# Packed queries in another engine order: when weight columns are copied, which accumulators are emptied first, and what lies between two spreads

## The chip, the cores and the metric

The kernel runs on one core of a Trainium2 chip. The metric is device time in microseconds (us), as the median of several executions; lower is better. The engines that matter are TensorE (PE in the profile, its weight loads PEld), ScalarE (ACT), VectorE (DVE), GpSimd (POOL) and SyncE (SP), which issues the DMAs. Each engine works off its own instructions in order.

## The reference

Four layers in a row, all in bf16 with 32-bit sums: linear attention (A), MLP (B), A, B, with the same weights for both A and both B. S = 2048 tokens, D = 576, F = 4608, 32 heads of 18 columns.

```python
phi = lambda t: jnp.where(t > 0, t + 1, jnp.exp(t)) + 1e-6
def A(y):                       # y: layernorm of x
    q, k, v = heads(y @ wqkv)   # 32 heads of 18
    pq, pk = phi(q), phi(k)
    kv = einsum("bhsd,bhse->bhde", pk, v)
    z = einsum("bhsd->bhd", pk)
    den = einsum("bhqd,bhd->bhq", pq, z)[..., None] + 1e-6
    return (einsum("bhqd,bhde->bhqe", pq, kv) / den) @ wo
def B(y):                       # y: layernorm of x
    return gelu(y @ w1 + b1) @ w2 + b2
x = x + A(ln(x)); x = x + B(ln(x)); x = x + A(ln(x)); x = x + B(ln(x))
```

## The kernel before, in words

**Order.** The order of TensorE's instructions is the order in which the program writes them (`pe(...)` chains each to the last). On the other engines a scheduler places the instructions, but manual dependencies (`tc.add_manual_dep(later, earlier, NOSYNC, ...)`, which order two instructions of one engine without a semaphore) and lists of names (`in_order`) fix it around the places at issue. All DMA loads of the beginning are chained on SP's queue. PSUM is cut into four single banks that go round as a ring (`ps_h`, tag "h") and two pairs of banks (`accA`, `accB`) for long sums. A ring tile waits until the last reader of the tile four places earlier is done.

**The attention layer.** It is linear attention without the usual products of values: instead of v it uses x^T phi(k). For each of 16 tiles of 128 tokens the keys are made in two halves of 288 columns (`k_half`, L731), phi is applied by ScalarE and VectorE, and `rows_by_keys` (L773) adds x^T times phi(k) for the first half of the keys into four 128-row blocks (k = 0 to 3, in `accA` and `accB`) and a block of the remaining 64 rows plus a row of sums (k = 4, the "tail", in a ring bank). Between them the queries are made: `q_proj(g, c)` for groups g = 0 to 3 of 128 columns (7 heads of 18 and two more columns) and blocks c of 512 tokens (L699), and for the group 4 of the 64 columns that are left, two blocks packed in one bank (L704).

**Packed queries.** Group 4 has 72 columns. Eight of them fill up the two free columns of each full group, so that a full group has 128: POOL copies them within the weight tile `wqkv_sb` (L240, two copies, called from `load_wq` at the beginning). In layer 0 the layernorm of a tile goes over VectorE's statistics, a power on POOL (`ln_rstd`, L477), two more steps on POOL, and then five transposes on TensorE (L549) with a copy on ScalarE; tiles from `XB` on are transposed by a DMA instead.

**After the last tile** come `last_rows_by_keys` (the tail block and the sums of the second half of the keys), `z_groups`/`z_tail`/`z_products` (the denominators' vectors), and the sums for the second half of the keys (`sums(n)`: n token tiles of `rows_by_keys`, four matmuls of 288 columns each), which are spread as filling between these steps: `den_stage` (L906: denominators of two blocks of 512 tokens), `quad_stage` and `scale_stage` (1/denominator for group 4), `quarter_stage(c)` (L949: 1/denominators of block c spread over the features by 16 small matmuls into all four ring banks, which ScalarE copies, L953, into the single buffer `turned`), `quarter_scale` (L959: VectorE multiplies the queries by it), `kv_groups` (L825: the weights of the values times the emptied sums `k2`, L758 and L756 being the copies that empty them), and `kv_wo_half(g, half)` (L854: kv times the output weights, one ring bank each; for group 4 copied out at L857 to L859, and eight rows of it sent to the other groups by four DMAs). Then `wo_products` (L1092) forms the output of the layer and `residual` (L675) adds x.

**The MLP layer** (L1207, L1271) follows with its own layernorms; `lnp.feed(..., hold=...)` says at which step of the attention layer's end a tile's layernorm may start.

Of the kernel before, what the change touches and what calls it, by code (L numbers as in the profile page):

```python
# [15 lines left out]
P = 128  # L16
NT = S // P
KD = 5
# [22 lines left out]
def build(tc, A_x, A_wqkv, A_wo, B_w1, B_b1, B_w2, B_b2, out, dbg=None, n_layers=4):  # L41
    nc = tc.nc
    dbg = dbg or {}
    with ExitStack() as ctx:
# [116 lines left out]
        XB = 7  # L161
# [68 lines left out]
        def load_wq():  # L230
# [7 lines left out]
            chained(nc.sync.dma_start(out=wqkv_sb[0:64, 4, GF4 * P:QW], in_=A_wqkv[4 * P:D, 0:GO[0]]))  # L238
            for n, ks in ((P, slice(0, 4)), (64, slice(4, 5))):
                nc.gpsimd.tensor_copy(  # L240
                    out=wqkv_sb[0:n, ks, 0:GF4 * P].rearrange("p k (g c) -> p k g c", g=GF4)[:, :, :, 126:P],
                    in_=wqkv_sb[0:n, ks, QW - 2 * GF4:QW].rearrange("p k (g c) -> p k g c", g=GF4))

# [140 lines left out]
        class LNPipe:  # L384
# [11 lines left out]
            def tick(self, transposes=1):  # L396
                land()
                for it in list(self.items):
# [69 lines left out]
                    elif st == 1:  # L468
# [8 lines left out]
                        nc.gpsimd.tensor_tensor(out=rstd[:], in0=it["u"][:], in1=neg_half[:], op=ALU.pow)  # L477
# [207 lines left out]
        def layer_A(li, next_kind, pre_a1=None):  # L685
# [65 lines left out]
            def plus_eps(engine, out, in_, eps):  # L751

                if li > 0:
                    (engine.copy if engine is nc.scalar else engine.tensor_copy)(out=out, in_=in_)
                elif engine is nc.scalar:
                    engine.activation(out=out, in_=in_, func=ACT.Identity, bias=eps)  # L756
                else:
                    engine.tensor_scalar(out=out, in0=in_, scalar1=eps, scalar2=None, op0=ALU.add)  # L758

            def rows_by_keys(t, half, chunks=(4, 0, 1, 2, 3), done=True):  # L760
# [14 lines left out]
                if summed and t == NT - 1:  # L775
# [4 lines left out]
                    for rows_, col in ((slice(0, 64), 4), (slice(64, 65), 5)):  # L780
                        nc.vector.tensor_scalar(out=key_eps[rows_, col:col + 1], in0=self_k["tail"][rows_, HALF:HALF + 1],
                                                scalar1=1e-6, scalar2=None, op0=ALU.mult)
                if 4 in chunks and t == NT - 1:
# [13 lines left out]
                if t < NT - 1:  # L797
                    return
                for i, engine in enumerate((nc.scalar, nc.vector)):
                    for j in range(2):  # L800
                        plus_eps(engine, k2[2 * i + j][:, cols], self_k["acc"][i][:, j, 0:HALF],
                                 key_eps[:, 2 * i + j:2 * i + j + 1])
# [15 lines left out]
            def kv_groups(groups):  # L818
# [3 lines left out]
                for g in groups:  # L822
                    cols = slice(GO[g], GO[g] + GR[g])
                    for k in range(KD):
                        pe(nc.tensor.matmul(ps[0:GR[g], start_of[g]:start_of[g] + GR[g]],  # L825
                                            lhsT=wqkv_sb[:, k, VO + GO[g]:VO + GO[g] + GR[g]],
                                            rhs=k2[k][:, cols], start=(g == groups[0] and k == 0), stop=(k == KD - 1),
# [23 lines left out]
            def kv_wo_half(g, half, by_dve=None):  # L851
# [4 lines left out]
                if g == GF4:  # L856
                    nc.vector.tensor_copy(out=kvwo["rest"][64:72, cols], in_=wp[64:72, 0:HALF])  # L857
                    nc.scalar.copy(out=kvwo[GF4][0:64, cols], in_=wp[0:64, 0:HALF])
# [523 lines left out]
```

## Time and profile before

| | |
|---|---|
| three runs | 760.76, 761.78, 762.96 us; median 761.78 |
| the profiled execution | 760.52 us; its span, first to last instruction, 758.8 us |
| granted TensorE clock | 1.000 over the span |
| busy | PE 745.7 us (98%), ACT 316.0 (42%), DVE 260.8 (34%), POOL 116.0 (15%) |
| attention layer 0, with the start | 0 to 102.18 us, PE busy 94.44 |
| MLP layer 1 | 102.18 to 384.01 us, PE busy 281.83 of 281.83 |
| attention layer 2 | 384.01 to 474.05 us, PE busy 87.64 of 90.04 |
| MLP layer 3 | 474.05 to 758.8 us, PE busy 281.83 of 284.75 |

How to read the rows. A row of the stretch table begins with the stretch in us, then its length, and the busy time with the count of instructions for PE, PEld, DVE, ACT and POOL; then the granted clock, the busy share of the DMA engines and GB/s. A row of the timeline begins with the start and the duration of a group of alike instructions, then engine, line, operation, output<-inputs, shapes and count; in brackets stands the idle time of that engine just before, and what ended it. In the chain, SPq, DVEq and so on are an engine's own queue. A row of the DMA list has destination<-source, the queue, the count and the size of one.

### The profile page before, as it was taken

The numbers are of one execution on the slowest core, as the hardware profiler recorded it, in microseconds if no ns is written. First come the engines' busy times: TensorE is split into PE (matmuls) and PEld (weight loads), VectorE is DVE, ScalarE is ACT, GpSimd is POOL, SyncE is SP. The second block draws the span as 40 slices with busy tenths as digits, with TensorE's granted clock in tenths as the row PEclk, the third lists the DMA queues.
The fourth block names the chain that finished last, engine by engine and source line by source line (L and its number), as shares of the span: only waits on it lengthen the run. The fifth ranks groups of instructions, "written<-read, shape, count | busy, mean of one in ns | idle before, by whom it ended". The sixth has DMA issues, their size and how long they took to land.

```text
span 758.8 us, 15697 instructions
## 1 busy us (share of the span) xinstructions
PE 745.7 (98%) x6531; PEld 474.7 (63%) x6531; DVE 260.8 (34%) x649; ACT 316.0 (42%) x706; POOL 116.0 (15%) x227
## 2 busy tenths in 40 slices
PE   8998999999999999999999999999999999999998
PEld 4665754774477457646776667457646754674476
DVE  6756844136023503401457577600230132000000
ACT  4666646205600650263057666660164036205600
POOL 4830402002000301300100004300020021001000
PEclk9999999999999999999999999999999999999999
DMA  8796694226302711320404137430240033011000
GB/s 224 188 250 138 201 320 143 67 63 188 84 35 83 181 51 48 107 67 21 137 24 118 42 112 273 171 83 16 79 111 20 16 125 83 9 32 56 2 9 24
DMA packets 89218, 75.89 MB, mean 100 GB/s; under 512 B 45674, under 2 KB 73786, under 8 KB 89146
## 3 DMA queue, kind: packets, MB, share of 16 engines
q1 hardware_dynamic: 89146, 74.88, 34.4%
q8 instruction: 51, 0.84, 0.5%
q14 instruction: 21, 0.17, 0.1%
HBM read 48.10 MB, written 24.77 MB: 96 GB/s over the span
## 4 chain that ended last, share of the span: by engine, by line
PE 91%; DVE 3%; ACT 2%; issue 1%; SPq 1%; POOL 1%; DMA 0%; DVEq 0%; POOLq 0%; ACTq 0%
PE m_ps L1271 36%; PE h_ps L1207 21%; PE hp_ps L1207 16%; PE wo_ps L1092 4%; PE k_ps L731 4%; PE q_ps L699 3%; PE k_ps L773 3%; ACT turned L953 1%; PE m_half L1271 1%; DVE pq L959 1%; PE q_ps L704 1%; PE k_tail L773 0%; PE rden_ps L949 0%; DMA wqkv_sb<-in_A_wqkv_dram 0%; SPq L234 0%
## 5 line engine op out<-in xcount | busy, mean ns | idle before, releaser
L1271 PE MATMUL m_ps<-w_sb,hT 128*128 128x288 bf16 x2232 | 274.8, 286 | 0.0
L1271 PEld LDWEIGHTS <-hT 128*128 128x128 bf16 x2304 | 224.3, 98 | 60.4 <-issue 3.4
L1207 PEld LDWEIGHTS <-w_sb 64*128 64x128 bf16 x2304 | 124.5, 94 | 136.4 <-issue 1.9
L1207 PE MATMUL hp_ps<-yT,w_sb 64*128 64x512 bf16 x1152 | 178.0, 376 | 0.0
L1207 PE MATMUL h_ps<-yT,w_sb 64*128 64x512 bf16 x1152 | 147.9, 376 | 0.0
L1212 ACT COPY relay_sb<-relay_sb 128x1 f32<-128x1 f32 x144 | 28.5, 198 | 261.3 <-PE h_ps L1207 218.7
L1203 ACT ACTIVATE hT<-h_ps,b1T 128x512 bf16<-128x512 f32 x144 | 91.1, 684 | 44.2 <-PE h_ps L1207 44.2
L477 POOL TENSOR_TENSOR ln_rstd<-ln_u,neg_half 128x1 f32<-128x1 f32 x62 | 34.8, 562 | 413.1 <-DVE ln_u L459 215.1
L1203 ACT ACTIVATE hT<-hp_ps,b1T 128x512 bf16<-128x512 f32 x144 | 91.2, 693 | 0.0
L675 DVE TENSOR_TENSOR xbf<-m_ps,xo 128x576 bf16<-128x576 f32 x15 | 11.4, 758 | 212.7 <-PE m_ps L1271 212.7
L675 DVE TENSOR_TENSOR xo<-m_ps,xo 128x576 f32<-128x576 f32 x16 | 12.1, 758 | 168.4 <-PE m_ps L1271 168.4
L658 POOL TENSOR_TENSOR xo<-xo,b_bc 128x576 f32<-128x576 f32 x32 | 40.9, 1282 | 105.8 <-DMA xo<-x_d 64.5
L1207 PE MATMUL h_ps<-yT,w_tail 64*128 64x512 bf16 x144 | 54.1, 376 | 0.0
L1207 PE MATMUL hp_ps<-yT,w_tail 64*128 64x512 bf16 x144 | 54.1, 376 | 0.0
L731 PE MATMUL k_ps<-wqkv_sb,yT 128*128 128x288 bf16 x320 | 44.5, 286 | 1.6 <-DMA yT<-x 1.2
L1092 PE MATMUL wo_ps<-kvwo,pq 128*128 128x288 bf16 x320 | 42.3, 286 | 0.0
L699 PE MATMUL q_ps<-yT,wqkv_sb 128*128 128x512 bf16 x160 | 39.6, 379 | 0.2
L731 PEld LDWEIGHTS <-yT 128*128 128x128 bf16 x320 | 30.9, 98 | 12.4 <-DMA yT<-x 1.5
L1207 PEld LDWEIGHTS <-w_tail 64*128 64x128 bf16 x288 | 27.1, 94 | 17.1
L1092 PEld LDWEIGHTS <-pq 128*128 128x128 bf16 x320 | 30.6, 98 | 8.4 <-issue 0.2
L621 ACT ACTIVATE phi_e<-q_ps 128x512 bf16<-128x512 f32 (+1 forms) x38 | 21.6, 574 | 24.2 <-PE q_ps L699 21.8
L340 DVE STREAM_TRANSPOSE turned<-y_ring 128x576 bf16<-128x576 bf16 x40 | 30.3, 766 | 0.4
(162 smaller groups left out, 541.7 us busy)
## 6 DMA issues: line engine op xcount, KB each, us to landing
xo<-x_d SPq DMA_DIRECT2D x48, 288.0 KB
x_d<-xo SPq DMA_DIRECT2D x32, 288.0 KB
xl<-x_d SPq DMA_DIRECT2D x24, 288.0 KB
y_d<-turned SPq DMA_DIRECT2D x40, 144.0 KB
w_sb<-in_B_w_dram SPq DMA_DIRECT2D x6, 864.0 KB
yT<-y_d SPq DMA_DIRECT2D x10, 512.0 KB
w_sb<-in_B_w_dram SPq DMA_DIRECT2D x9, 512.0 KB
x_d<-xn SPq DMA_DIRECT2D x16, 288.0 KB
```

The costliest lines, as they stand in the source:

```text
L340: turn = nc.vector.transpose(out=turned[:, :, j, :], in_=y[:, 0:D])
L477: nc.gpsimd.tensor_tensor(out=rstd[:], in0=it["u"][:], in1=neg_half[:], op=ALU.pow)
L658: nc.gpsimd.tensor_tensor(out=xo[:], in0=xo[:], in1=b2_bc[:], op=ALU.add)
L675: total = nc.vector.tensor_tensor(out=xn[:, cols].rearrange("p (h n) -> p h n", h=2), in0=halves, in1=xo[:, cols].rearrange("p (h n) -> p ...
L699: pe(nc.tensor.matmul(qp[:], lhsT=wqkv_sb[:, k, g * P:(g + 1) * P], rhs=yT[:, k, c * CA:(c + 1) * CA], start=(k == 0), stop=(k == KD - 1)))
L731: pe(nc.tensor.matmul(kp[:, 0:HALF], lhsT=yT[:, k, t * P:(t + 1) * P], rhs=wqkv_sb[:, k, KO + half * HALF: KO + (half + 1) * HALF], start= ...
L773: pe(nc.tensor.matmul(dst, lhsT=lhsT, rhs=pk, start=(t == 0), stop=(t == NT - 1)))
L1092: pe(nc.tensor.matmul(wp[:, half, 0:HALF], lhsT=features, rhs=kvwo[slot][:, half * HALF:(half + 1) * HALF], start=(g == WO_ORDER[0]), stop ...
L1203: act_last["gelu"] = nc.scalar.activation(out=to, in_=ps, func=ACT.Gelu_apprx_tanh, bias=b1T[:, f:f + 1], scale=1.0).ins.name
L1207: mm = pe(nc.tensor.matmul(dst[n], lhsT=wt, rhs=mv, start=(seen[n] == 0), stop=(seen[n] == 8)))
L1212: relay = nc.scalar.copy(out=relay_sb[:, 1:2], in_=relay_sb[:, 0:1])
L1271: pe(nc.tensor.matmul(acc[half][:, 0:cols.stop - cols.start], lhsT=hT[f][:, j * P:(j + 1) * P], rhs=w2_sb[:, f, cols], start=(f == 0), sto ...
```

## The change

- **Weight columns.** The two copies of L240 are taken out of `load_wq` into a function `fill_groups`, which is called later, after `load_wqkv(2)` (the loads of the values' weights) and after the keys of tile 2. Manual dependencies put them behind the last power on POOL and one behind the other, the power of tile 4 behind them, and each power of a layer-0 tile behind POOL's last normalization.
- **XB** goes from 7 to 8: tile 7 is transposed on TensorE.
- **Long accumulators first.** In `rows_by_keys` of the last tile the copies that empty `accA` and `accB` are written ahead of those of the tail, and ScalarE's copies are held in this order.
- **kv by key blocks.** `kv_groups` loops over the key blocks (0, 1, 4, 2, 3) outside and over the groups inside.
- **Denominators.** `den_stage` runs its two blocks inside the loop over the groups.
- **Last group.** `kv_wo_half(4, ...)` copies its 72 rows once, by VectorE, into `rest`, and after the second half POOL copies 64 rows from there to each of the two tiles of group 4. The second spread, `quarter_stage(1)`, stands ahead of `kv_wo_half(4, 0)` instead of behind `kv_wo_half(4, 1)`, and `sums` are dealt out otherwise. `last_rows_by_keys` stands ahead of `z_groups(0, 1)` and `z_tail`.
- **hold** of token tile 2 in the attention layer 2 is 8 instead of 6.

```diff
@@ -158,7 +158,7 @@
         y_ring = [const.tile([P, DPAD], BF16, name=f"y_ring{i}") for i in range(NY)]
         key_eps = const.tile([P, 8], F32, name="key_eps")
         AHEAD = 4
-        XB = 7
+        XB = 8
         BY_ACT = (10, 13)
         turned = const.tile([P, D // 32, TPC, 32], BF16, name="turned")
         x_d = dpool.tile([NT, P, D], F32, name="x_d")
@@ -236,10 +236,14 @@
             chained(nc.sync.dma_start(out=wqkv_sb[:, 0:4, GF4 * P:QW],
                                       in_=A_wqkv[0:4 * P, 0:GO[0]].rearrange("(k p) n -> p k n", p=P)))
             chained(nc.sync.dma_start(out=wqkv_sb[0:64, 4, GF4 * P:QW], in_=A_wqkv[4 * P:D, 0:GO[0]]))
+
+        def fill_groups():
             for n, ks in ((P, slice(0, 4)), (64, slice(4, 5))):
-                nc.gpsimd.tensor_copy(
+                filled = nc.gpsimd.tensor_copy(
                     out=wqkv_sb[0:n, ks, 0:GF4 * P].rearrange("p k (g c) -> p k g c", g=GF4)[:, :, :, 126:P],
                     in_=wqkv_sb[0:n, ks, QW - 2 * GF4:QW].rearrange("p k (g c) -> p k g c", g=GF4))
+                tc.add_manual_dep(filled.ins, first_ones["fill"].ins.name if "fill" in first_ones else pool_last["pow"], NOSYNC, reason="tiles go on first")
+                first_ones["fill"] = filled
 
         nc.scalar.preload_act_table_set("natural_log_exp_and_others")
         load_x0(0)
@@ -474,7 +478,12 @@
                             named(f"re{it['t']}", nc.scalar.activation(out=rstd[:], in_=rstd[:], func=ACT.Exp, scale=-0.5))
                             it["stage"] = 2
                             continue
-                        nc.gpsimd.tensor_tensor(out=rstd[:], in0=it["u"][:], in1=neg_half[:], op=ALU.pow)
+                        power = nc.gpsimd.tensor_tensor(out=rstd[:], in0=it["u"][:], in1=neg_half[:], op=ALU.pow)
+                        pool_last["pow"] = power.ins.name
+                        if it["kind"] == "A" and it["norm"] == "pool" and pool_last["norm"] is not None:
+                            tc.add_manual_dep(power.ins, pool_last["norm"], NOSYNC, reason="tiles one by one")
+                        if it["t"] == 4 and "fill" in first_ones:
+                            tc.add_manual_dep(power.ins, first_ones.pop("fill").ins.name, NOSYNC, reason="queries' weights first")
                     elif st == 2 and it["norm"] != "dve":
                         nmr = work.tile([P, 1], F32, name="ln_nmr", bufs=4)
                         nc.gpsimd.tensor_scalar(out=nmr[:], in0=it["mv"][:, 0:1], scalar1=1.0 if it["stats"] == "act" else -1.0,
@@ -751,11 +760,15 @@
             def plus_eps(engine, out, in_, eps):
 
                 if li > 0:
-                    (engine.copy if engine is nc.scalar else engine.tensor_copy)(out=out, in_=in_)
+                    step = (engine.copy if engine is nc.scalar else engine.tensor_copy)(out=out, in_=in_)
                 elif engine is nc.scalar:
-                    engine.activation(out=out, in_=in_, func=ACT.Identity, bias=eps)
+                    step = engine.activation(out=out, in_=in_, func=ACT.Identity, bias=eps)
                 else:
-                    engine.tensor_scalar(out=out, in0=in_, scalar1=eps, scalar2=None, op0=ALU.add)
+                    step = engine.tensor_scalar(out=out, in0=in_, scalar1=eps, scalar2=None, op0=ALU.add)
+                if engine is nc.scalar:
+                    if act_last.get("k2") is not None:
+                        tc.add_manual_dep(step.ins, act_last["k2"], NOSYNC, reason="banks of the sums first")
+                    act_last["k2"] = step.ins.name
 
             def rows_by_keys(t, half, chunks=(4, 0, 1, 2, 3), done=True):
 
@@ -780,6 +793,11 @@
                     for rows_, col in ((slice(0, 64), 4), (slice(64, 65), 5)):
                         nc.vector.tensor_scalar(out=key_eps[rows_, col:col + 1], in0=self_k["tail"][rows_, HALF:HALF + 1],
                                                 scalar1=1e-6, scalar2=None, op0=ALU.mult)
+                if done and t == NT - 1:
+                    for i, engine in enumerate((nc.scalar, nc.vector)):
+                        for j in range(2):
+                            plus_eps(engine, k2[2 * i + j][:, cols], self_k["acc"][i][:, j, 0:HALF],
+                                     key_eps[:, 2 * i + j:2 * i + j + 1])
                 if 4 in chunks and t == NT - 1:
                     nc.gpsimd.memset(zk[:, cols], 0.0)
                     plus_eps(nc.scalar, k2[4][0:64, cols], self_k["tail"][0:64, 0:HALF], key_eps[0:64, 4:5])
@@ -794,12 +812,6 @@
                     del row_of[t]
                     if li == 0 and t == NT - 1:
                         x0_tiles.clear()
-                if t < NT - 1:
-                    return
-                for i, engine in enumerate((nc.scalar, nc.vector)):
-                    for j in range(2):
-                        plus_eps(engine, k2[2 * i + j][:, cols], self_k["acc"][i][:, j, 0:HALF],
-                                 key_eps[:, 2 * i + j:2 * i + j + 1])
 
             def last_rows_by_keys():
 
@@ -819,12 +831,12 @@
 
                 ps = ps_h.tile([P, 512], F32, name="kv_ps", tag="h")
                 start_of = {g: 126 * i for i, g in enumerate(groups)}
-                for g in groups:
-                    cols = slice(GO[g], GO[g] + GR[g])
-                    for k in range(KD):
+                for k in (0, 1, 4, 2, 3):
+                    for g in groups:
+                        cols = slice(GO[g], GO[g] + GR[g])
                         pe(nc.tensor.matmul(ps[0:GR[g], start_of[g]:start_of[g] + GR[g]],
                                             lhsT=wqkv_sb[:, k, VO + GO[g]:VO + GO[g] + GR[g]],
-                                            rhs=k2[k][:, cols], start=(g == groups[0] and k == 0), stop=(k == KD - 1),
+                                            rhs=k2[k][:, cols], start=(g == groups[0] and k == 0), stop=(k == 3),
                                             skip_group_check=True))
                 full = [g for g in groups if g < GF4]
                 n = len(full)
@@ -854,10 +866,10 @@
                 pe(nc.tensor.matmul(wp[0:GR[g], 0:HALF], lhsT=kvT[0:GR[g], g, 0:GR[g]],
                                     rhs=wo_sb[0:GR[g], g, cols], start=True, stop=True))
                 if g == GF4:
-                    nc.vector.tensor_copy(out=kvwo["rest"][64:72, cols], in_=wp[64:72, 0:HALF])
-                    nc.scalar.copy(out=kvwo[GF4][0:64, cols], in_=wp[0:64, 0:HALF])
-                    nc.vector.tensor_copy(out=kvwo[GF4 + 1][64:P, cols], in_=wp[0:64, 0:HALF])
+                    nc.vector.tensor_copy(out=kvwo["rest"][0:72, cols], in_=wp[0:72, 0:HALF])
                     if half:
+                        for hi in range(2):
+                            nc.gpsimd.tensor_copy(out=kvwo[GF4 + hi][64 * hi:64 * (hi + 1), :], in_=kvwo["rest"][0:64, :])
                         for i in range(GF4):
                             nc.sync.dma_start(out=kvwo[i][126:P, :], in_=kvwo["rest"][64 + 2 * i:66 + 2 * i, :])
                     return
@@ -899,12 +911,13 @@
             def den_stage(c):
 
                 dp = ps_h.tile([P, 512], F32, name="den_ps", tag="h")
-                for i in range(2):
-                    for g in range(G):
+                for g in range(G):
+                    for i in range(2):
                         for j in range(TPC):
                             features, slot = tile_of(g, c + i, j)
                             pe(nc.tensor.matmul(dp[32 * j:32 * (j + 1), i * P:(i + 1) * P], lhsT=zsel[:, slot, :],
-                                                rhs=features, start=(g == 0), stop=(g == G - 1)))
+                                                rhs=features, start=(g == 0 and i == 0), stop=(g == G - 1),
+                                                skip_group_check=True))
                 rden = work.tile([P, 2, P], BF16, name="rden", bufs=1)
                 nc.scalar.activation(out=dp[:, 2 * P:4 * P], in_=dp[:, 0:2 * P], func=ACT.Ln, bias=key_eps[:, 7:8])
                 act_last["rden"] = nc.scalar.activation(out=rden[:].rearrange("p i n -> p (i n)"), in_=dp[:, 2 * P:4 * P],
@@ -981,6 +994,7 @@
                 phi()
                 rows_by_keys(0, 0, (0, 1, 2, 3), done=False)
                 keys(2)
+                fill_groups()
                 feed_and_tick(4, 2)
                 rows_by_keys(1, 0, (0, 1, 2, 3), done=False)
                 rows_by_keys(2, 0, (0, 1, 2, 3), done=False)
@@ -1038,10 +1052,10 @@
                         rows_by_keys(t - 1, 0)
                 rows_by_keys(NT - 1, 0)
 
+            last_rows_by_keys()
+            left = list(range(NT))
             z_groups(0, 1)
             z_tail()
-            last_rows_by_keys()
-            left = list(range(NT))
             z_groups(1, 3)
 
             def sums(n):
@@ -1058,25 +1072,24 @@
             quad_stage(0)
             sums(2)
             quarter_stage(0)
-            sums(1)
+            sums(2)
             kv_groups((4, 0))
             scale_stage(0)
             quarter_scale(0, (0, 1, 2, 3), after=dve_last["quad"])
             q_proj(*q_left.pop(0))
             kv_wo_tiles()
+            sums(3)
+            quarter_stage(1)
+            sums(1)
             kv_wo_half(4, 0)
-            sums(2)
+            sums(1)
             kv_wo_half(4, 1)
-            sums(1)
-            quarter_stage(1)
-            sums(2)
             quarter_scale(1, (0, 1, 2, 3), after=dve_last["quad"])
             q_proj(*q_left.pop(0))
             sums(1)
             kv_wo_half(0, 0)
             sums(1)
             kv_wo_half(0, 1)
-            sums(1)
 
             wo_open = {}
 
@@ -1101,7 +1114,7 @@
                     if li == 0:
                         hold, tp_at, by_act = ((2, 0, 4, 6)[t], (5, 7, 8, 12)[t], t in (1, 2))
                     else:
-                        hold, tp_at, by_act = ((2, 5, 6, 8)[t], (6, 9, 11, 13)[t], t in (1, 2))
+                        hold, tp_at, by_act = ((2, 5, 8, 8)[t], (6, 9, 11, 13)[t], t in (1, 2))
                     lnp.feed(xn, t, "B", "pool", "xbar" if li == 0 and t < 3 else "act", hold=hold, tp_at=tp_at,
                              **(dict(stats="act", after="rden") if by_act else dict(after="sum")))
```

## The prediction

> **What bounds the kernel.** I read the page first (busy shares, then the chain that ended last), next the table of stretches for TensorE's idle time, and last the timeline around each hole.
>
> ```profile
> span 758.8 us, 15697 instructions
> PE 745.7 (98%) x6531; PEld 474.7 (63%) x6531; DVE 260.8 (34%) x649; ACT 316.0 (42%) x706; POOL 116.0 (15%) x227
> PE 91%; DVE 3%; ACT 2%; issue 1%; SPq 1%; POOL 1%; DMA 0%; DVEq 0%; POOLq 0%; ACTq 0%
> ```
> ```profile
> 12.00:16.00 4.00, 2.76 (x25) 2.10 (x26) 2.84 (x9) 1.30 (x4) 1.69 (x8) 1.00 0.93 261
> 56.00:60.00 4.00, 3.35 (x43) 2.01 (x42) 3.03 (x14) 3.96 (x10) 0.00 (x0) 1.00 1.09 358
> 68.00:72.00 4.00, 2.55 (x32) 1.68 (x30) 2.70 (x8) 1.89 (x6) 1.40 (x3) 1.00 0.01 3
> 439.00:443.00 4.00, 2.55 (x32) 1.65 (x31) 2.39 (x7) 1.89 (x5) 0.00 (x0) 1.00 0.26 75
> ```
> TensorE carries 91% of the chain and is idle 13.1 us in all (758.8 - 745.7). In the stretch rows the third number is its busy time: 1.24 us are missing in 12 to 16, 0.65 in 56 to 60, 1.45 in 68 to 72 and again in 439 to 443. The change is aimed at these holes; it can win a few us at most, and a new hole in TensorE costs its full length.
>
> **Part 1, the start: tile 3 and the copied weight columns.**
>
> ```profile
> 10.31 1.39 PE L731 MATMUL k_ps<-wqkv_sb,yT 128*128 128x288 bf16 x10
> 11.60 0.21 POOL L240 COPY wqkv_sb<-wqkv_sb 128x32 bf16<-128x32 bf16 x1 [3.57 <-DMA wqkv_sb<-in_A_wqkv_dram]
> 12.18 0.54 POOL L477 TENSOR_TENSOR ln_rstd<-ln_u,neg_half 128x1 f32<-128x1 f32 x1
> 13.24 0.45 PE L549 MATMUL tp<-ident,x 128*128 128x128 bf16 x5 [1.54 <-DVE x L490]
> 15.08 0.38 SPq L223 DMA_DIRECT2D wqkv_sb<-in_A_wqkv_dram  x1
> 15.15 0.55 POOL L477 TENSOR_TENSOR ln_rstd<-ln_u,neg_half 128x1 f32<-128x1 f32 x1 [2.21 <-DVE ln_u L459]
> 15.74 1.24 PE L699 MATMUL q_ps<-yT,wqkv_sb 128*128 128x512 bf16 x5
> 15.77 0.46 DVE L601 SCALAR_TENSOR_TENSOR pk<-k_ps,y_ring 128x288 bf16<-128x288 f32 x1 [0.34 <-ACT y_ring L599]
> 16.93 0.34 POOL L784 MEMSET y_ring<- 128x288 bf16 x1
> 17.05 0.45 PE L549 MATMUL tp<-ident,x 128*128 128x128 bf16 x5
> ```
> Before, POOL sits 3.57 us in front of the copy, so tile 3's power (12.18) is late and TensorE waits 1.54 us for tile 3. In the changed order that power stands ahead of the copies and needs only statistics that are ready: the 1.54 us go, and TensorE would reach the first `q_proj` at 14.2 instead of 15.74.
>
> What is late next is the copy itself. It now stands after `load_wqkv(2)` in the program, and in the built program its wait list has grown: on one DMA semaphore it asks for four completions instead of two, and the fourth is the load of the values' weights (L223, issued at 15.08). The copy doesn't read them; their rows interleave with its own. POOL is in order, so behind the copy stand tile 4's power, its two norm steps, and with them TensorE's transposes of tile 4 and everything after; the first `q_proj` reads the copied columns too.
>
> When does that load land? No view prints it, so bounds:
>
> ```profile
> 15.00:19.00 4.00, 3.94 (x28) 2.24 (x26) 3.41 (x12) 2.80 (x6) 2.87 (x7) 1.00 0.95 289
> 19.00:22.50 3.50, 3.50 (x30) 2.50 (x29) 3.47 (x12) 2.42 (x6) 2.69 (x8) 1.00 1.06 303
> 22.50:23.00 0.50, 0.50 (x7) 0.40 (x5) 0.50 (x4) 0.50 (x2) 0.02 (x1) 1.00 0.51 162
> 23.00:25.00 2.00, 2.00 (x18) 1.32 (x16) 1.72 (x7) 1.49 (x4) 1.79 (x3) 1.00 0.16 52
> w_sb<-in_B_w_dram SPq DMA_DIRECT2D x9, 512.0 KB
> wqkv_sb<-in_A_wqkv_dram SPq DMA_DIRECT2D x1, 576.0 KB
> wqkv_sb<-in_A_wqkv_dram SPq DMA_DIRECT2D x3, 72.0 KB
> ```
> Last columns: DMA share and GB/s. Behind the 576 KB come two of 72 KB and two of 512 KB, 1.196 MB in all. After 23 some 0.10 MB still move, in 22.5 to 23 0.08, so 1.01 MB move before 22.5; at 303 GB/s the 576 KB are through at 19.2 if all DMA engines keep step. They don't: traffic halves at about 22.75 and ends near 25, so the last engine trails by some 2.2 us. Bounds 19.2 and 25; I take 19.2 + 2.2 = 21.4, since the load needs its slowest engine. The Trainium skill (DMA: Bandwidth & Descriptors, "Why a DMA increments its semaphore by 16 and not by 1") says that engines finish independently and only the full 16 means landed, which is the later reading; no row here shows the sixteen one by one.
>
> From 21.4 on: both copies until 21.9 (0.2 us each by L240), power of tile 4 at 22.0, and from power to transpose 1.90 us as before (15.15 to 17.05): 23.9, that is 6.9 us later than 17.05. The saved 1.54 us drown in this wait; so would the memset L784, now ahead of the copies.
>
> TensorE then stands idle from 14.2 to 21.7. What a restart costs shows at the kernel's beginning:
>
> ```profile
> 1.05 3.65 PE L263 MATMUL warm_ps<-y_ring 128*128 128x512 bf16 x9 [1.05 <-DVE y_ring L258]
> 5.61 0.59 PE L263 MATMUL warm_ps<-y_ring 128*128 128x512 bf16 x2
> 30.89 1.08 PE q_ps L699 x5
> 137.25 35.39 PE m_ps L1271 x288
> ```
> After rest, 512-column matmuls took 0.406 us each for 3.65 us; running, they take 0.216 (1.08/5). If 7.5 us of rest are enough for that, the first 3.65 us from 21.7 run at about half speed. Up to 23.9 this is hidden (tile 4 isn't there); of the other 1.5 us half is lost, 0.8 us (0 if it doesn't happen, 1.2 if slow until 5.61 in the row above). The Trainium skill (TensorE: Matmul & The Clock Gate, "Part 1: The HAM clock gate") puts the clock back to half after an idle window of about 3.4 us and asks for about as long a busy one; by it the restart is slow. The longest hole in this trace is too short to show it. Start in all: **+7.7 us**.
>
> **Part 2, tile 7 through TensorE (`XB` 8): 0.**
>
> ```profile
> 28.49 1.40 PE L731 MATMUL k_ps<-wqkv_sb,yT 128*128 128x288 bf16 x10 [1.19 <-DMA yT<-x]
> 30.11 0.28 PE L773 MATMUL k_tail<-pk,x 128*65 128x289 bf16 x1 [0.22 <-POOL pk L737]
> ```
> The 1.19 us wait for the transposing DMA goes, for five transposes (about 0.3) and one more copy on ScalarE. But the step after it already waits for POOL, which has no pause there, so the end at 30.11 stays. At best 0.6 us are won.
>
> **Part 3, from the sums to the last queries, in both attention layers.**
>
> ```profile
> 59.61 1.74 PE L773 MATMUL k_ps<-pk,x 128*128 128x288 bf16 x12 [0.65 <-ACT k L756]
> 64.15 0.40 PE L949 MATMUL rden_ps<-rden,head_bc 32*128 32x128 bf16 x16
> 64.57 2.05 ACT L953 CAST turned<-rden_ps 128x512 bf16<-128x512 f32 x4 [0.47 <-PE rden_ps L949]
> 69.08 0.23 PE L949 MATMUL rden_ps<-rden,head_bc 32*128 32x128 bf16 x2
> 70.61 0.76 PE L949 MATMUL rden_ps<-rden,head_bc 32*128 32x128 bf16 x14 [1.30 <-DVE kvwo L859]
> 76.94 0.85 PE L825 MATMUL kv_ps<-k,wqkv_sb 128*126 128x126 bf16 x12 [0.21 <-DVE k L758]
> 77.72 1.27 PE L704 MATMUL q_ps<-yT,wqkv_sb 128*64 128x512 bf16 x10
> 434.84 0.41 PE L949 MATMUL rden_ps<-rden,head_bc 32*128 32x128 bf16 x16
> 448.28 1.27 PE L704 MATMUL q_ps<-yT,wqkv_sb 128*64 128x512 bf16 x10
> 69.28 1.20 POOL L849 MEMSET kvwo<- 64x576 bf16 x2
> ```
> Accumulators first: in layer 0 ScalarE empties them before the tails, 0.8 us sooner; the 0.65 us wait goes but for about 0.05 (VectorE's two). The vector zk comes when it came, since the same four copies lie before `z_rows`. Gain 0.6, layer 0 alone.
>
> From the first spread (64.15) to L704 (77.72) are 13.57 us. Work in it: 40 matmuls of 288 columns at 0.123 (35.39/288) = 4.9, 16 of 512 at 0.216 = 3.5, two spreads at about 0.33 = 0.7, 25 of 72 or 126 columns at 0.065 (12 in 76.94 to 77.72) = 1.6: 10.7. So 2.9 us are waits, 2.8 in layer 2 (13.44): mainly the second spread, which needs four banks while two hold `kvwo_half` of group 4. Moved ahead of that group, it finds its banks free. Three waits are new: `kvwo_half(4, 0)` and the next `q_proj` take banks that ScalarE's four spread copies (0.51 each by L953) free, about 0.2 and 0.3 us; kv's second key block waits about 0.2 for ScalarE's copy. Left: 2.3 (layer 0) and 2.1 (layer 2). With the 0.6: **-5.0 us**; bounds -3.5 (each new wait twice over) and -6.1 (none).
>
> At nothing: the denominators' order (the same 40 matmuls); group 4's copies on POOL, each between 0.60 (L849) and 0.85, ready by about 72.5, while L704, ahead of which no product of group 4 is formed, stands at 77.72; the kvwo DMAs behind two more `xo` loads in layer 2, whose banks of keys are summed by then; the `hold` of tile 2, which moves no instruction on TensorE or ScalarE. If the cover of the DMAs or of POOL were gone, each us late costs one us in its layer.
>
> **Sum.** The profiled execution took 760.52 us (1.72 beside its span); 760.5 + 7.7 - 5.0 = 763.2. The median of the three runs, 761.78, is 1.26 above it: **764.5**.
>
> **The rivals.**
> - The wait on the values' weights doesn't bind (the load lands by 15). For it: nobody in the trace waits for that load, so its landing is unseen. Against: 1.2 MB queue behind it and traffic is full until 22.5. Then the copies wait for L601's last read of `y_ring` (now about 14.7) and the memset, tile 4 comes 0.4 late, and the time is 761.8 + 0.4 - 5.0 = 757.2.
> - The clock stays up through the hole: 763.7. For it: no row shows a fall.
> - ScalarE's spread copies become the bound of part 3: the second set may start only when VectorE has read the one buffer `turned`. It decides if VectorE's first scalings end later than about 68.5; TensorE then stands as it stood for L859, the gain shrinks to 2, and the time is 767.5. Against it: TensorE's waits there name L859, not a copy of ScalarE, and from 64.57 to 68.5 is time for more scalings than the four that free `turned`; so I hold it unlikely.
>
> **How the numbers follow.** The forecast has 0.50, the steady clock 0.27, the ScalarE bound 0.15, the missing wait 0.08. A measurement of this kernel tells about 0.3% (2.3 us) from no change, so "same" is 759.5 to 764.1. Faster: the missing wait, 0.08. Same: most of the steady clock and a good quarter of the forecast, if the load lands sooner, 0.34. Slower: 0.58. The range lets the landing move by a us either way and takes in both restarts and part 3's lower bound: 761.3 to 767.7.
>
> **What would show it.** Right: POOL's copy of the columns near 21.5 with a long wait on a DMA, TensorE idle some 7 us ahead of the first `q_proj` and its matmuls there near 0.4 us, tile 4's transposes near 24; layer 0's MLP starting 4 to 6 us later than 102.2 (less layer 0's 2.9 gained), no wait on L859, and layer 2's attention some 2 us shorter. Wrong: the copy at 12 to 16, or no hole ahead of the first `q_proj`.

## The result and the profile after

The changed kernel takes 763.89 us (median of 16 runs, 762.96 to 765.16), the kernel before 761.93 us (16 runs, 760.65 to 763.12): a ratio of 1.0026, 95% interval 1.0018 to 1.0034. So it is slower by 0.26%, with an interval clear of 1, but 763.89 still lies inside the 759.5 to 764.1 us that the prediction called "same" and gave 0.34; the "slower" that it held likelier, at 0.58, begins above that. The forecast of 764.5 us and its range held; the steps behind it did not all hold, and two of the misses offset each other.

The page of the changed kernel, its span and its busy shares:

```profile
span 762.8 us, 15695 instructions
PE 748.5 (98%) x6536; PEld 475.8 (62%) x6536; DVE 261.1 (34%) x645; ACT 315.0 (41%) x703; POOL 119.3 (16%) x231
```

The timeline of its start (POOL and TensorE; L242 is the copy that was L240, L708 the `q_proj` that was L699, L558 the transposes, L786 the sums, L740 the keys):

```profile
21.81 0.33 POOL L242 COPY wqkv_sb<-wqkv_sb 128x32 bf16<-128x32 bf16 x2 [6.73 <-DMA w_sb<-in_B_w_dram]
22.08 2.31 PE L708 MATMUL q_ps<-yT,wqkv_sb 128*128 128x512 bf16 x5 [7.73 <-POOL wqkv_sb L242]
24.19 0.74 PE L558 MATMUL tp<-ident,x 128*128 128x128 bf16 x5
26.86 0.88 PE L786 MATMUL k_ps<-pk,x 128*128 128x289 bf16 x4
27.57 1.39 PE L740 MATMUL k_ps<-wqkv_sb,yT 128*128 128x288 bf16 x10
36.52 1.40 PE L740 MATMUL k_ps<-wqkv_sb,yT 128*128 128x288 bf16 x10 [0.17 <-ACT yT L564]
38.79 0.28 PE L786 MATMUL k_tail<-pk,x 128*65 128x289 bf16 x1 [0.88 <-POOL pk L746]
```

POOL's copy stands behind 6.73 us of waiting for a DMA, and TensorE behind the copy for 7.73 us. The row names a load of MLP weights (`w_sb`), which the copy doesn't use; such names are inferred, and the times of the completions that the trace keeps say which load it was. The load of the values' weights (L223, issued at 15.28) reports sixteen completions, from 19.03 to 21.69 us, and the copy starts at 21.81; the load named in the row had only begun to report at 21.72 and ended at 23.69. In two of the runs below the copy starts 0.12 us behind the last of the same sixteen as well (e2: 21.83 behind 21.71; e3: 21.41 behind 21.29), and in e3 its row names `wqkv_sb`:

```profile
21.41 0.33 POOL L242 COPY wqkv_sb<-wqkv_sb 128x32 bf16<-128x32 bf16 x2 [6.49 <-DMA wqkv_sb<-in_A_wqkv_dram]
```

Tile 4's transposes come 7.14 us later than before (24.19 against 17.05), and the sums behind them 8.44 us later (26.86 against 18.42, first row of the next fence but one): between those two TensorE itself was slow. The stretches show it (the granted clock, the share of its full speed at which TensorE was let run, is the third number from the end):

```profile
16.00:17.00 1.00, 0.00 (x0) 0.00 (x0) 0.17 (x2) 0.00 (x0) 0.00 (x0) 1.00 0.92 260
17.00:18.00 1.00, 0.00 (x0) 0.00 (x0) 0.00 (x0) 0.00 (x0) 0.00 (x0) 0.53 0.92 295
27.00:27.50 0.50, 0.50 (x5) 0.30 (x4) 0.00 (x0) 0.40 (x1) 0.00 (x0) 0.70 0.00 0
27.50:28.00 0.50, 0.50 (x6) 0.40 (x5) 0.27 (x2) 0.50 (x2) 0.00 (x0) 1.00 0.00 0
```

The clock falls to half inside the hole, at 17.06 (0.53 over a microsecond of which 0.94 are at half), and comes back at 27.30, 5.2 us after TensorE has started again.

How far the changed kernel lies behind at each stage is read from the first row of the same work in both. Before:

```profile
18.42 0.66 PE L773 MATMUL k_ps<-pk,x 128*128 128x289 bf16 x4
18.91 1.39 PE L731 MATMUL k_ps<-wqkv_sb,yT 128*128 128x288 bf16 x10
57.18 0.67 PE L812 MATMUL z_rows<-pk,x 128*32 128x288 bf16 x16
102.11 1.04 PE L1207 MATMUL h_ps<-yT,w_sb 64*128 64x512 bf16 x8
428.69 0.67 PE L812 MATMUL z_rows<-pk,yrow_pair 128*32 128x288 bf16 x16
473.98 1.04 PE L1207 MATMUL h_ps<-yT,w_sb 64*128 64x512 bf16 x8
```

After (the third row is the packed last group, L704 before; the last row is the stretch with the second spread; in that of before, 68 to 72, TensorE was busy 2.55 of 4 us):

```profile
66.00 0.67 PE L824 MATMUL z_rows<-pk,x 128*32 128x288 bf16 x16
76.97 0.40 PE L962 MATMUL rden_ps<-rden,head_bc 32*128 32x128 bf16 x16
83.87 1.27 PE L713 MATMUL q_ps<-yT,wqkv_sb 128*64 128x512 bf16 x10
108.30 1.04 PE L1220 MATMUL h_ps<-yT,w_sb 64*128 64x512 bf16 x8
434.95 0.67 PE L824 MATMUL z_rows<-pk,yrow_pair 128*32 128x288 bf16 x16
452.56 1.27 PE L713 MATMUL q_ps<-yT,wqkv_sb 128*64 128x512 bf16 x10
478.03 1.04 PE L1220 MATMUL h_ps<-yT,w_sb 64*128 64x512 bf16 x8
76.00:80.00 4.00, 3.89 (x40) 2.32 (x38) 2.50 (x8) 2.75 (x6) 1.58 (x4) 1.00 0.00 0
```

At layer 0's `z_rows` it is 8.82 us behind, at the packed last group 6.15, at the first MLP 6.19; in layer 2 it goes from 6.26 to 4.28, and ends 4.0 behind (762.8 against 758.8). So the start costs 8.8 us and the ends of the two attention layers give back 4.8. The second spread (76.97) now runs as one piece of 16 matmuls with no wait ahead of it.

Between the medians lie only 2.0 us, not 4.0. The profile of before was one of its quickest executions (760.52 us against a median of 761.93), the profile after is above its own median (764.52 against 763.89): 4.0 - 1.4 - 0.6. Where these 1.4 us come from is the subject of e9 and e12.

### The profile page after: what moved, and what is told of

Same layout as the page of the kernel before. It is cut to its first block, busy times and chain, and to the rows that moved or that the text cites. A ratio compares the mean times of both kernels' runs of the same rounds, so it can differ in the third digit from the quotient of the medians.

```text
span 762.8 us, 15695 instructions
## 1 busy us (share of the span) xinstructions
PE 748.5 (98%) x6536; PEld 475.8 (62%) x6536; DVE 261.1 (34%) x645; ACT 315.0 (41%) x703; POOL 119.3 (16%) x231
## 4 chain that ended last, share of the span: by engine, by line
PE 93%; SPq 1%; ACT 1%; DMA 1%; DVE 1%; POOL 1%; issue 1%; POOLq 0%; ACTq 0%; DVEq 0%
PE m_ps L1284 36%; PE h_ps L1220 20%; PE hp_ps L1220 16%; PE wo_ps L1105 5%; PE q_ps L708 4%; PE k_ps L740 4%; PE k_ps L786 3%; PE m_half L1284 1%; SPq L214 1%; DMA w_sb<-in_B_w_dram 1%; PE q_ps L713 1%; DMA wqkv_sb<-in_A_wqkv_dram 1%; ACT turned L966 1%; PE k_tail L786 0%; PE rden_ps L962 0%
## 5 line engine op out<-in xcount | busy, mean ns | idle before, releaser
L708 PE MATMUL q_ps<-yT,wqkv_sb 128*128 128x512 bf16 x160 | 41.8, 395 | 7.7 <-POOL wqkv_sb L242 7.7
L740 PE MATMUL k_ps<-wqkv_sb,yT 128*128 128x288 bf16 x320 | 44.6, 286 | 0.2 <-ACT yT L564 0.2
L740 PEld LDWEIGHTS <-yT 128*128 128x128 bf16 x320 | 30.9, 98 | 11.4 <-issue 0.6
```

What stands on the lines that cost most here:

```text
L708: pe(nc.tensor.matmul(qp[:], lhsT=wqkv_sb[:, k, g * P:(g + 1) * P], rhs=yT[:, k, c * CA:(c + 1) * CA], start=(k == 0), stop=(k == KD - 1)))
L740: pe(nc.tensor.matmul(kp[:, 0:HALF], lhsT=yT[:, k, t * P:(t + 1) * P], rhs=wqkv_sb[:, k, KO + half * HALF: KO + (half + 1) * HALF], start= ...
```

## The experiments

**e1: the copies without the wait.** The changed kernel with the two copies called where they were before, ordered by hand behind tile 3's power and ahead of tile 4's.

```diff
 def load_wq():
     ...
+    for n, ks in ((P, slice(0, 4)), (64, slice(4, 5))):
+        first_ones[f"fill{n}"] = nc.gpsimd.tensor_copy(...)
-                fill_groups()
+    if it["t"] == 3: add_manual_dep(fill128, power of tile 3); add_manual_dep(fill64, fill128)
+    if it["t"] == 4: add_manual_dep(power of tile 4, fill64)
```

> The changed kernel, but with the two copies of weight columns called where they were before (so that they come ahead of the loads of the values' weights in the program and have no overlap with them to wait for), and ordered behind the power of tile 3 and ahead of the power of tile 4. Theory: the hole of 7.7 us is the wait for the landing of the values' weights and nothing else; the copies then run near 11.8, the first q_proj of TensorE starts near 14.3, its matmuls take 0.216 us each, and the time is that of before less what the later parts win in the profile (0.7 + 1.9 + 2.1 = 4.7) and less 0 to 1.5 of tile 3's wait: 755.7 to 757.2. Rival: the copies are late because of their place on POOL (behind tile 3's power, tiles one by one): then a hole of several us stays and the time is above 760.

754.08 us (753.97 to 754.43; ratio to before 0.9896, interval 0.9882 to 0.9909), granted clock 1.000 in each run. Its timeline, POOL and TensorE at the start, then the stages:

```profile
11.89 0.33 POOL L240 COPY wqkv_sb<-wqkv_sb 128x32 bf16<-128x32 bf16 x2 [1.06 <-DMA wqkv_sb<-in_A_wqkv_dram]
14.16 1.24 PE L707 MATMUL q_ps<-yT,wqkv_sb 128*128 128x512 bf16 x4
15.24 0.44 PE L557 MATMUL tp<-ident,x 128*128 128x128 bf16 x5
28.46 0.28 PE L785 MATMUL k_tail<-pk,x 128*65 128x289 bf16 x1 [0.93 <-POOL pk L745]
56.15 0.67 PE L823 MATMUL z_rows<-pk,x 128*32 128x288 bf16 x16
74.01 1.27 PE L712 MATMUL q_ps<-yT,wqkv_sb 128*64 128x512 bf16 x10
424.87 0.67 PE L823 MATMUL z_rows<-pk,yrow_pair 128*32 128x288 bf16 x16
442.47 1.27 PE L712 MATMUL q_ps<-yT,wqkv_sb 128*64 128x512 bf16 x10
```

The copies run at 11.89, with the place on POOL behind tile 3's power kept, and the hole is gone: the place costs nothing, the later landing costs all. At `z_rows` of layer 0 e1 is 9.85 us ahead of the changed kernel (56.15 against 66.00), which is the whole difference between their medians (9.8). It also beats the expectation, by 1.6 us; the sum of the stages (1.0 at `z_rows`, 5.1 behind it) explains the profile, 752.7 against 758.8, and the rest of the 8.2 us between the medians is that before's median beside it (762.29) stands 1.8 above its profile. One more thing differs from the changed kernel: POOL's memset of `y_ring`, ahead of the copies there, has come to stand behind tile 4's norm.

**e2: TensorE kept busy in the hole.** The changed kernel with matmuls ahead of the first `q_proj`.

```diff
 qp = ps_h.tile([P, 512], F32, name="q_ps", tag="h")
+if li == 0 and (g, c) == (0, 0):
+    for _ in range(30):
+        pe(nc.tensor.matmul(qp[:], lhsT=yT[:, 0, 0:P], rhs=yT[:, 0, 0:CA], start=True, stop=True))
```

> The changed kernel with 30 more matmuls of 512 columns (on tiles already there, into the bank of the first q_proj, which overwrites them) ahead of the first q_proj: at 0.216 us each they fill 14.3 to 20.8 of the hole. Theory: the slow matmuls from 22.1 to 27.2 come from TensorE's rest alone, so they run at full speed from 22.1, tile 4's transposes still come near 24.2, and the 1.3 to 1.5 us lost behind them come back: 762.4 to 762.6, granted clock 1.000. Rival: the slow matmuls come from something else in the same stretch (weights or tiles still landing): granted clock and time as in the changed kernel, 763.9.

761.91 us (11 runs; ratio to before 1.0002, 0.9993 to 1.0012): 2.0 us less than the changed kernel, for thirty matmuls more, and 0.5 under the range expected. The granted clock is 1.000 in ten runs and 0.999 in one.

```profile
22.10 1.25 PE L711 MATMUL q_ps<-yT,wqkv_sb 128*128 128x512 bf16 x5 [1.65 <-POOL wqkv_sb L242]
25.38 0.66 PE L789 MATMUL k_ps<-pk,x 128*128 128x289 bf16 x4
```

The copy ends when it did, `q_proj` starts when it did, but its five matmuls take 1.25 instead of 2.31 us, and the sums come at 25.38 instead of 26.86. Rest alone makes the matmuls slow, and that costs 1.5 to 2.0 us.

**e3 and e4: each half alone.** e3 is the kernel before with `fill_groups` and the powers' dependencies; e4 the changed kernel without them and with `XB` at 7.

> The kernel before with the first part alone: the later copies and the new dependencies of the powers on POOL; tile 7 by DMA as before, everything behind the keys as before. Theory: all of the loss is here. By the profiles of before and after the first z_rows of layer 0 comes 8.8 us later, so 770.7; by the medians (2.0 over before with 4.7 won later) 6.7 later, so 768.6. Rival (part of the loss comes from XB or the later parts): under 768.

> The changed kernel with its first part and XB undone: only accumulators first, kv by key blocks, denominators' order, last group behind the spread, hold. Theory: the parts are independent and it wins 4.7 (0.7 + 1.9 in layer 0, 2.1 in layer 2): 757.2, and no wait of TensorE on the copy of the last group. Rival: the later parts won only because layer 0 had come later and its transfers were all there: under 3 us won, above 759.

e3 took 768.73 us (ratio 1.0093, 1.0076 to 1.0110), e4 756.72 us (0.9929, 0.9915 to 0.9943). So the start loses 6.4 us against the median of before and the ends win 5.6, 0.8 more than by the profile. Together that is 0.9 us lost, where the changed kernel lies 1.6 above the same median (762.29): the halves don't add up exactly, and why is not shown. The profile of e4 shows something that the profile of before does not (timeline of TensorE, then stretches with TensorE, clock, DMA):

```profile
13.62 0.45 PE L550 MATMUL tp<-ident,x 128*128 128x128 bf16 x5 [2.07 <-DVE x L491]
14.97 2.61 PE L732 MATMUL k_ps<-wqkv_sb,yT 128*128 128x288 bf16 x10
11.41:14.82 3.41, 1.34 (x15) 1.00 0.92 246
14.82:18.22 3.40, 3.19 (x13) 0.50 0.98 295
```

Its start is that of before, with a hole of 2.07 us in front of tile 3 instead of 1.54. After that hole, with TensorE already at work again, the clock is at half for 3.40 us, and ten matmuls take 2.61 us instead of 1.39.

**e5, e6: the order or the copies.** Both start from e1. e5 puts the second spread and the sums back where they stood, e6 the last group's three copies (diffs shortened).

```diff
 e5:  quarter_stage(0)
-     sums(2)
+     sums(1)
      ... kv_wo_tiles()
-     sums(3); quarter_stage(1); sums(1)
      kv_wo_half(4, 0)
-     sums(1)
+     sums(2)
      kv_wo_half(4, 1)
+     sums(1); quarter_stage(1); sums(2)
      ... kv_wo_half(0, 1)
+     sums(1)
 e6:
-     nc.vector.tensor_copy(out=kvwo["rest"][0:72, cols], in_=wp[0:72, 0:HALF])
-     ... nc.gpsimd.tensor_copy(out=kvwo[GF4 + hi][...], in_=kvwo["rest"][0:64, :])
+     nc.vector.tensor_copy(out=kvwo["rest"][64:72, cols], in_=wp[64:72, 0:HALF])
+     nc.scalar.copy(out=kvwo[GF4][0:64, cols], in_=wp[0:64, 0:HALF])
+     nc.vector.tensor_copy(out=kvwo[GF4 + 1][64:P, cols], in_=wp[0:64, 0:HALF])
```

> The kernel of e1 (754.08 us, clock 1.000 in every run), with one thing put back: the second spread and the sums stand where they stood before, behind both halves of the last group's products. Theory: the 1.9 and 2.1 us won come from the place of the second spread, since it finds four free banks ahead of the last group; with it put back TensorE waits again for the copy of the last group ahead of the second spread, 0.7 to 1.3 us in each attention layer, and the time is 755.5 to 758. Rival: the gain comes from the fewer copies of the last group (one instead of three readers of a bank): then the wait is under 0.3 us and the time under 754.7.

> The kernel of e1 with the copies of the last group as before (two by VectorE, one by ScalarE, none by POOL), the second spread still ahead of it. Theory: where the spread stands decides, so the time stays within 0.4 us: 753.9 to 754.5. Rival: the copies decide: 1 to 2 us more.

e5 took 755.50 us, e6 754.06. The three copies cost nothing where the spread stands early. With the spread late and one copy, TensorE waits twice, 0.41 us in all, not 0.7 to 1.3 (timeline of e5, layer 0):

```profile
67.19 0.21 PE L961 MATMUL rden_ps<-rden,head_bc 32*128 32x128 bf16 x1 [0.26 <-DVE kvwo_rest L868]
67.56 0.38 PE L961 MATMUL rden_ps<-rden,head_bc 32*128 32x128 bf16 x13 [0.15 <-DVE kvwo_rest L868]
```

Layer 2 has another 0.4 us of this wait. Both together make 0.8 us, while e5's median lies 1.4 above e1's; the other 0.6 are not explained by it. Neither theory stands alone: either edit takes away most of the wait. e12 puts both back.

**e7, e8, e10, e11: the small parts.** All start from e1. e7 empties the accumulators behind the tails, e8 sets `XB` to 7, e10 moves three memsets behind tiles 6 to 8 from POOL to VectorE, e11 loops kv over groups first (diffs shortened).

```diff
 e7:
-    if done and t == NT - 1: ... plus_eps(engine, k2[...], self_k["acc"][i][...])   # ahead of the tails
+    if t == NT - 1: ... the same copies, behind the tails
 e10:
+    if t in (6, 7, 8): nc.vector.memset(pk[:, HALF:HALF + 1], 1.0)
 e11:
-    for k in (0, 1, 4, 2, 3):
-        for g in groups:
+    for g in groups:
+        for k in range(KD):
```

> The kernel of e1 with the accumulators emptied behind the tails as before. Theory: the wait of 0.65 us ahead of the first sums of layer 0 comes back and nothing else: 754.6 to 754.8, and TensorE waits on the copy of ScalarE there. Rival: 754.1, the wait was there only because layer 0 was earlier.

> The kernel of e1 with tile 7 transposed by DMA as before. Theory: POOL's memset behind tile 7 holds TensorE in both cases, so the time is the same within 0.3 us: 753.8 to 754.6, a wait on the DMA of about 1.2 us in place of most of the wait of 0.93 on POOL. Rival: the DMA comes later than POOL and 0.6 us or more are lost: above 754.7.

> The kernel of e1 with the memsets of the column of ones for tiles 6 to 8 on VectorE instead of POOL. Theory: the 0.93 us that TensorE waits on POOL behind tile 7 go, and what comes next there is VectorE's own product of tile 7 (its inputs come from TensorE 1.5 us earlier), so 0.3 to 0.9 us are won: 753.2 to 753.8. Rival: another step of POOL (a later tile's norm) or ScalarE is late next and nothing is won: 754.0.

> The kernel of e1 with kv by groups as before instead of by key blocks. Theory: the copies of the sums are ready by then with the second spread early, so it costs at most the 0.2 us that TensorE waited on VectorE's copy (layer 0): 754.1 to 754.4. Rival: the order by key blocks is what lets kv start, and 0.5 us or more are lost in each layer: above 755.

They took 755.12 (e7), 754.09 (e8), 754.25 (e10) and 754.93 us (e11), against 754.08. e1 ran on another chip than these and e5, e6 and e12; the kernel before, at clock 1.000, has medians of 760.9 to 761.2 us on the three chips, so a difference of 0.3 us says nothing here. A row or two each: e7's first sums (timeline), e8's wait for the DMA, and e11's waits of kv (lists of waits: us in total, times, longest):

```profile
58.38 1.74 PE L781 MATMUL k_ps<-pk,x 128*128 128x288 bf16 x12 [0.65 <-ACT k L764]
PE k_ps L739 <- DMA yT<-x: 1.3, 1, 1.3
PE kv_ps L836 <- DVE k L766: 0.7, 2, 0.5
PE kv_ps L836 <- DVE k L762: 0.5, 1, 0.5
```

e7: the wait of 0.65 us is back, 1.0 us by the medians (its runs go from 754.52 to 756.57). e8: one wait changes places with the other and the time stays, as expected. e10: the wait on POOL is gone from its profile, whose run took 753.25 us, but the other three took 754.18 to 754.52, so no gain is shown. e11: the theory fell. Kv by groups makes TensorE wait 1.2 us on VectorE's copies, over both layers, and costs 0.85 us; where the second spread stands early, the order by key blocks is a gain.

**e9: the hole of tile 3 filled in the kernel before.**

```diff
 tp = ps_h.tile([P, 512], F32, name="tp", tag="h")
+if first_layer and t == 3:
+    for _ in range(6):
+        pe(nc.tensor.matmul(tp[:], lhsT=yT[:, 0, 0:P], rhs=wqkv_sb[:, 0, KO:KO + 512], start=True, stop=True))
```

> The kernel before with six more matmuls of 512 columns ahead of the transposes of tile 3 (into their bank, which they overwrite); at 0.216 us they take 1.3 us, less than the hole there. Theory: the runs of before at 762 to 764 are those in which the clock falls for a stretch after that hole (1.5 us in its profile, 2.1 in that of e4), so with the hole filled the granted clock is 1.000 in every run and the median that of before's runs with clock 1.000: 760.7 to 761.3. Rival: the spread of before's runs comes from the DMA: clock 0.995 to 0.998 in half the runs, median 762.

761.97 us (12 runs; ratio 1.0004, 0.9994 to 1.0013), and the clock is below 1.000 in 7 of 12 runs. The theory fell for this place: filling the hole of tile 3 changes nothing. But the profile shows where the clock falls instead (timeline of TensorE; stretches with TensorE, clock, DMA):

```profile
71.44 0.77 PE L952 MATMUL rden_ps<-rden,head_bc 32*128 32x128 bf16 x14 [1.30 <-DVE kvwo L862]
73.28 2.34 PE L702 MATMUL q_ps<-yT,wqkv_sb 128*128 128x512 bf16 x5
69.55:72.96 3.41, 1.97 (x27) 1.00 0.01 3
72.96:76.38 3.42, 3.42 (x13) 0.50 0.33 89
```

Behind the wait of the second spread, the very one that the change removes, the clock is at half for 3.42 us; TensorE had been busy 1.97 of the 3.41 us before. Layer 2 has the same at 445 to 448.5. That these falls are what lengthens before's slower runs is read from their clocks, since its one profile has none. The runs of before, 49 of them beside e1 to e12, split without overlap: with the clock at 1.000 (17 runs) 760.66 to 761.53 us, median 761.05; below it (32 runs) 761.68 to 763.94, median 762.30.

**e12: e5 and e6 together**, so the spread late and three copies.

> The kernel of e1 with both put back that e5 and e6 put back singly: the second spread behind the last group, and that group's three copies as before. Theory: either edit alone takes most of the wait (e5 left 0.4 us of it in each layer, e6 none), both together bring back the waits of 1.3 us in each attention layer, so the profile is 3.5 to 4.2 us above e1's 752.7 where the clock stays up; and since the holes of about 1.5 us that these waits make are where the clock fell in e9 (near 73 and 443), the granted clock is under 1.000 in a third or more of the runs, each fall costing about 1.7 us: median 757.5 to 760. Rival: the clock falls in before for another reason (the start): clock 1.000 in every run, median 757.5 to 758.2. Second rival: the copies do not matter, and the time is that of e5, 755.5.

757.13 us (6 runs, 756.59 to 759.75). The wait is back, and against e1 the way from `z_rows` to the packed group is 1.41 us longer in layer 0 and 1.53 in layer 2:

```profile
55.77 0.67 PE L823 MATMUL z_rows<-pk,x 128*32 128x288 bf16 x16
68.45 0.76 PE L961 MATMUL rden_ps<-rden,head_bc 32*128 32x128 bf16 x14 [1.30 <-DVE kvwo L870]
75.04 1.27 PE L712 MATMUL q_ps<-yT,wqkv_sb 128*64 128x512 bf16 x10
425.83 0.67 PE L823 MATMUL z_rows<-pk,yrow_pair 128*32 128x288 bf16 x16
444.01 1.02 PE L836 MATMUL kv_ps<-k,wqkv_sb 128*126 128x126 bf16 x15
444.96 1.27 PE L712 MATMUL q_ps<-yT,wqkv_sb 128*64 128x512 bf16 x10
```

Three runs at clock 1.000 took 756.59 to 757.34 us, two at 0.998 and 0.995 took 759.52 and 759.75, and the profiled one (756.93) stood at 0.999, with no fall between 6.93 and 754.4 us. So two runs of six fell, where none of the 28 runs of e1, e5 to e8, e10 and e11, which have these waits short or not at all, lies below 0.999. That speaks for the holes of the spread; the place of the fall is seen only in the profile of e9, since the two runs of e12 left no profile, and of five runs of e3, which has the same waits, only one has a lower clock than the others (0.991 against 0.995). My price in the expectation was a microsecond too high: the order of kv, which e12 keeps, carries that part. From kv to the packed group it takes 0.95 us in layer 2 (444.01 to 444.96) where before took 1.41 (446.87 to 448.28), and 1.02 where before took 1.55 in layer 0:

```profile
446.87 1.48 PE L825 MATMUL kv_ps<-k,wqkv_sb 128*126 128x126 bf16 x15
```

## Why the prediction came out right, and where its steps were wrong

- **The wait on the values' weights: right.** The copy came at 21.81 (forecast 21.4), tile 4's transposes 7.14 us later (6.9), TensorE idle 7.73 us (7.5). The copy stands 0.12 us behind the last completion of the load that the prediction named, the fourth on that semaphore; in before's trace the same load is complete at 21.43 us, though no row prints it. e1 shows that this landing is the whole cause, and e3 that the start alone carries the loss.
- **The clock's restart: right mechanism, term too small.** It entered with 0.8 us; the profiles give 1.3 at the sums (8.44 less 7.14) and 1.5 at tile 4's keys (27.57 against 18.91 is 8.66, less 7.14), above the 1.2 that it gave as the worst, and e2 gives 2.0 by the medians. I let the slow stretch last 3.65 us from the restart; it lasted 5.2. The start in all came to 8.8 us, not 7.7.
- **Tile 7: right.** Its keys came 0.6 us nearer (36.52 against 28.49, 8.03 behind instead of 8.66) and the next step lost it again to POOL's memset (38.79 against 30.11, 8.68); e8 finds no difference.
- **Accumulators first: right**, 0.6 forecast; the stage gave 0.72, e7 0.65 by its wait.
- **The ends: right sum, wrong parts.** Forecast 5.0, measured 4.8 between the profiles. (By its own terms the sum is 4.9, since 2.9 less the three new waits leaves 2.2 in layer 0, and its upper bound 6.3; neither changes the forecast much.) But I gave the gain to the spread's place and counted the order of kv as a new wait of 0.2 us. e12 gives the spread with its copies 1.4 and 1.5 us, and e11 gives the order of kv about 0.85 over both layers. And the place alone is not what does it: one copy instead of three leaves 0.4 us of the 1.3 with the spread late (e5). These parts make 4.5 with the accumulators; 0.3 is not placed.
- **From the profile to the median: wrong, and it offset the rest.** I added 1.26 us because before's median lay that far above its profile, as if this were a constant. It is a clock fall that before has in two runs of three, and e9 and e12 speak for the change taking it away with the spread's holes; the changed kernel's median even lies 0.6 us below its profile, whose slow stretch was one of the longer ones (clock 0.993, as in 6 of 16 runs, median 764.4; the other ten at 0.996, median 763.7). The start 1.1 and the ends 0.2 too low, the offset 1.9 too high: that is how 764.5 lands 0.6 above 763.89. So close a hit is luck: the start and the ends taken alone come out 1.3 us too low.
- **The rivals.** "No wait" was priced at 757.2; built as e1 it gives 754.1, since nothing of tile 3's gain is lost (e1 is 1.0 ahead of before at `z_rows`, the rival 0.4 behind), and before's offset goes too. That the memset's place saves tile 3's gain is likely, but was not tried by itself. "The clock stays up" is e2: 761.9. ScalarE's spread copies did not become the bound: no wait in the changed kernel's list for TensorE, 0.2 us or longer, names them.

What stays open: how many of before's clock falls belong to the hole of tile 3 and how many to the spreads (e4 has the first alone, and 1 of 5 runs with a fall; e12 the second alone, and 2 of 6). The denominators' order and the hold of tile 2 were not tried by themselves.

## What to carry to other kernels

Where a copy on an in-order engine is moved later in a program, look at what its wait list has gathered on the way: a load that it doesn't read can cost the whole landing of that load, and calling the copy earlier while keeping its order by hand costs nothing (754.08 against 763.89 us). Why the copy was made to wait for it, by rows that interleave with its own as the prediction says, was not tried by itself. Read a median that lies above its own profile as a sign of something that only some executions have, and look at the granted clock of each run before adding the difference to a forecast. Short holes in TensorE are dearer than their length where the clock can fall behind them: before's runs with and without a fall lie 1.2 us apart by their medians.

## What the runs showed of the hardware

TensorE's clock falls for whole pieces of one length. The slow stretches last 3.40 us (e4), 3.42 (e9), 6.83 (e3) and 10.24 (the changed kernel, three times 3.41), and they don't begin and end with TensorE's rest: in the changed kernel the fall comes 2.7 us after the rest begins (14.35 to 17.06), and the clock comes back 5.2 us after the work does. The Trainium skill (TensorE: Matmul & The Clock Gate, "Part 1: The HAM clock gate") gives a free-running window of 3413 ns, and these lengths agree with it. It also says that the clock goes to half after at least one idle window; here the measurements differ: in the 3.41 us before the fall TensorE was busy 0.71 us in the changed kernel, 1.34 in e4 and 1.97 in e9, in the last two with holes of 2.07 and 1.30 us. The same hole lets the clock fall in some executions and not in others: the wait of 1.30 us ahead of the second spread stands in the profile of before too, at clock 1.000 throughout. Nor does the busy time of such a piece decide alone: before has pieces of 3.41 us with 1.86 and 1.96 us of work (from 11.03 and from 69.06) and no fall behind them. What decides stays open.
